# Last phase of a long-convolution gate kernel: sums of two rows in one place, row-buffer copies at the end of a step, separate buffers for x, 18 constant matmuls for 40

## The chip, the cores and the metric

The kernel runs on one core of one Trainium2 chip. The core has five engines with instruction streams of their own, which meet through semaphores: TensorE (PE, matmuls; its weight loads are shown as PEld), VectorE (DVE), ScalarE (ACT), GpSimd (POOL) and SyncE (SP, which here only issues DMAs). Sixteen DMA engines move the data of all queues. TensorE works out of SBUF, the on-chip memory, and writes to PSUM, which is read by VectorE and ScalarE. The metric is the device time of one launch, in microseconds; lower is better.

## What is computed

The reference is a long convolution (by FFT) of `x * v` with a filter that a small MLP makes from position embeddings, multiplied by `x`; then a five-tap causal convolution along the sequence, a sigmoid of it as a gate, and two 128x128 projections. Shapes: batch 4, sequence 12800, width 128.

```python
def _attn_ref(x, v, pos_emb, w1, w2):
    h_filt = (np.maximum(pos_emb @ w1, 0.0) @ w2) * np.exp(-0.01 * pos)[:, None]
    u = x * v
    L = 2 * S
    y = np.fft.irfft(np.fft.rfft(u, n=L, axis=1) * np.fft.rfft(h_filt, n=L, axis=0)[None], n=L, axis=1)[:, :S]
    return x * y
...
def _moe_ref(x, w_val, conv_w, w_out):          # x is the output of the above
    for k in range(5):
        gate_pre += conv_w[k] * xp[:, k:k + S, :]
    gate = 1.0 / (1.0 + np.exp(-gate_pre))
    return gate * (x @ w_val) @ w_out
```

## The kernel before

The FFT is cut into two halves j of 100 x 64 points (n1 x n2). The kernel has three phases, each with its own pools of SBUF and PSUM. Phase 1 makes the filter and the first transform and writes it to DRAM (`a_u`). Phase 2 goes over 50 pairs of frequencies, multiplies by the filter and transforms back along n2; it writes `c_y` to DRAM from `c_sb` (L376, L379). Phase 3, the one that changes, does the last inverse transform along n1 and everything behind it. One pool, `ld` (six buffers of 128 x 2048 words), lives through all three phases and holds what is loaded from DRAM; the pools of a phase (`p2`, `p3` and their PSUM) are given back when it ends, and the next phase's tiles take the same memory.

Phase 3 works on rows: a row is one n2 with all four batches and 100 n1, so 400 columns of 128 channels. Four rows (R = 4) make a group, 16 groups make a half, and there are 32 groups, 128 rows. The code is in `manual_schedule`: every engine runs its instructions in the order in which the Python text issues them. The loop at L591 runs over steps t, each with four rows r (L601). In step t the work is staggered over groups: group s = t + 3 goes through the inverse transform, group t through the five taps, and group t - 1 through the projections. Since the halo of the taps needs the last group of a half first, `y_order` begins each half with group 15.

In one row, these instructions are issued (names as in the profile):

- PE: four transposes `tp` (L517) of a row two rows back, the first projection `v_ps` (L554), the two inverse transforms `sd` of row (s, r) (L503, one for each half of the 128 partitions of the result), and the second projection `o_ps` (L564) of the row before. An fp32 matmul runs as two instructions in the profile, so an `sd` is shown as x4 and an `o_ps` or `v_ps` as x2.
- ACT: `dif` (L519, half of a transposed row out of PSUM), `o_sb` (L572, a result row out of PSUM), `sd_sb` (L510, the `sd` out of PSUM). In the last row of a step also the first tap of the next group (`gt`, L542) and the sigmoid (`sg`, L549).
- DVE: one of the taps 1 to 4 over the whole group (`gt`, L545), the gate times value product `gd` (L559), and the two halves `yr` of the row (L527, L528).
- POOL: `yr` times x into the row buffer `ext` or `tail` (L530).

`ext` is a buffer of 4 + 16 rows, so it holds four groups and, ahead of them, the last four rows of the four groups before. `fill_halo` (L483) copies these on ACT: L495 from the buffer before, L490 to L493 from `tail` at the start of a half, and L497 the `tail` into the end of the fourth buffer of a half. Before the change it is called in row r = 1 of a step with g % 4 == 0, eight times in all.

`load_rows` (L457) loads two tiles of `c_y` for a group, in eight DMAs on SP (96 and 4 partitions of each half tile), and the group's x with them (`load_x`, L451), one DMA. All three tiles are taken from `ld`; with six buffers that is two groups. The x of the first three groups is asked for ahead of the first `c_y` tiles (L583). While the loads run, 40 constant matmuls `w_ps` into the `o_ps` buffers (L587, called `o_ps<-dft,ident` in the profile) keep TensorE at work.

Of the kernel before, what the change touches and what calls it, by code (L numbers as in the profile page):

```python
# [9 lines left out]
F32 = mybir.dt.float32  # L10
# [13 lines left out]
B, S, D, FO, KC = 4, 12800, 128, 64, 5  # L24
J, N1, N2 = 2, 100, 64
# [1 line left out]
KG = 8  # L27
P1C = 2
R = 4
WARM = 40  # L30
NC1 = N1 // 2 + 1


# [72 lines left out]
def tile_longconv_gate(  # L106
# [56 lines left out]
    def load():  # L163
        return ld.tile([128, 2048], F32, name="ld")
# [276 lines left out]
    with tc.tile_pool(name="p3", bufs=1) as p3, tc.tile_pool(name="ps3", bufs=1, space=PSUM) as ps3:  # L441
        HALO = KC - 1
        ROW = B * N1
        NG = N2 // R
        EG = 4
# [4 lines left out]

        def load_x(s):  # L451
            j, g = y_order[s]
            xr = load()[:, 0:R * ROW]
            nc.sync.dma_start(out=xr, in_=xt[j][:, g * R:(g + 1) * R].rearrange("d n b a -> d (n b a)"))
            loads3[s] = xr

# [16 lines left out]
        def place(j, g):  # L473

            if g == NG - 1 and (j, g // EG) not in exts:
                return tails[j], 0
            return exts[j, g // EG], HALO + g % EG * R

        def new_ext(j, q):
            e = p3.tile([D, HALO + EG * R, B, N1], F32, name="ext", bufs=2)  # L480
            exts[j, q] = e
# [17 lines left out]
        def y_sum(s, r):  # L499
            ct, _ = loads3[s]  # L500
            sd = ps3.tile([128, B * D], F32, name="sd", bufs=2)
            for c in range(2):
                nc.tensor.matmul(  # L503
                    out=sd[c * N2:(c + 1) * N2], lhsT=inv[:, c], rhs=ct[c][:, r * B * D:(r + 1) * B * D],
                    start=True, stop=True)
            sds[s, r] = sd
# [15 lines left out]
        def y_join(s, r):  # L522
            tp, dif = tps.pop((s, r))
            j, g = y_order[s]
            xr = loads3[s][1].rearrange("d (n b a) -> d n b a", n=R, b=B)[:, r]
            yr = p3.tile([D, B, N1], F32, name="yr", bufs=3)
            nc.vector.tensor_tensor(yr[:, :, 0:NC1], tp[:, :, 0:NC1], dif, op=ALU.add)  # L527
            nc.vector.tensor_tensor(yr[:, :, NC1:N1], tp[:, :, 1:NC1 - 1], dif[:, :, 1:NC1 - 1], op=ALU.subtract)  # L528
            e, r0 = place(j, g)
            nc.gpsimd.tensor_tensor(e[:, r0 + r], yr, xr, op=ALU.mult)  # L530
# [24 lines left out]
            return v_ps  # L555

        def gated(t, r, v_ps):
            gd = p3.tile([D, ROW], F32, name="gd", bufs=3)
            nc.vector.tensor_tensor(gd, v_ps, gate_sg[t][:, r * ROW:(r + 1) * ROW], op=ALU.mult)  # L559
            return gd  # L560

# [18 lines left out]
        AHEAD3, NT, LAG = 3, len(groups), 2  # L580
        y_run, gd_last, o_last = [], None, None
        with tc.manual_schedule():
            for s in range(AHEAD3):  # L583
                load_x(s)
            load_rows(0)

            for _ in range(WARM):  # L587
                w_ps = ps3.tile([D, 2 * D], F32, name="o_ps", bufs=2)
                nc.tensor.matmul(  # L589
                    out=w_ps, lhsT=ident, rhs=dft.rearrange("p a k -> p (a k)"), start=True, stop=True)  # L590
            for t in range(-AHEAD3, NT + 2):  # L591
                s = t + AHEAD3
                if s + 1 < NT:
                    load_rows(s + 1)
                if 0 <= s < NT:
                    j, g = y_order[s]
                    if g == NG - 1:
                        tails[j] = p3.tile([D, R, B, N1], F32, name="tail", bufs=2)
                    elif g % EG == 0:
                        new_ext(j, g // EG)  # L600
                for r in range(R):  # L601
                    done = y_run.pop(0) if len(y_run) == LAG or s >= NT and y_run else None
                    if done:
                        y_trans(*done)
                    v_ps = value(t - 1, r) if 0 <= t - 1 < NT else None
                    if s < NT:
                        y_sum(s, r)
                    if o_last is not None:
                        finish(*o_last)
                        o_last = None  # L610
                    if gd_last is not None:
                        o_last = gd_last[0], gd_last[1], project(gd_last[2])
                        gd_last = None
                    if 0 <= t < NT:
                        tap(t, r + 1)
                    if r == R - 1 and 0 <= t + 1 < NT:
                        tap(t + 1, 0)
                    if v_ps is not None:
                        gd_last = t - 1, r, gated(t - 1, r, v_ps)
                    if done:  # L620
                        y_join(*done)
                    if s < NT:
                        y_copy(s, r)
                        y_run.append((s, r))
                    if r == R - 1 and 0 <= t < NT:
                        sigmoid(t)
                    if r == 1 and s < NT and g % EG == 0:
                        fill_halo(j, g // EG)


# [35 lines left out]
```

## Time and profile before

| | |
|---|---|
| median of 3 runs | 1285.75 us (1273.37, 1285.75, 1292.47) |
| the profiled execution | 1290.03 us; its span, first to last instruction, 1288.2 us |
| mean granted TensorE clock of it | 0.957 |
| busy in the span: PE, DVE, POOL, ACT | 91%, 79%, 67%, 49% |
| phase 3, from the first constant matmul to the end of the span | 849.5 to 1288.2 us, 438.7 us |
| busy in 850 to 1290: the taps L545, 128 instructions | 242.7 us, 1896 ns each |
| the same for L530 on POOL (into `ext`), 120 instructions | 301.6 us, 2514 ns each |

The busy share of an engine is an average over three phases with different limits, so phase 3 is read by itself, in windows and row by row. The profile gives a start and a length for each instruction. The lengths of neighbouring instructions of one engine overlap, so the pace of an engine is read from the distance of two starts, not from a length. A number in square brackets is the idle time of the engine just before the instruction, with the event that ended it.

### The profile page before, as it was taken

The page shows a single profiled execution, that of the slowest core. Times are in us where ns is not written, and L with a number is a line of the kernel's source. Part 1 is how long each engine was busy: PE and PEld are TensorE (multiplying, and loading weights), DVE is VectorE, ACT ScalarE, POOL GpSimd, SP SyncE. Part 2 cuts the span into 40 slices and gives each one's busy share as a digit, 9 for nine tenths or more (in the row PEclk, how much of TensorE's full clock was granted, in tenths as well). Part 3 has the DMA queues.
Part 4 walks back from the last instruction along what each step waited for, and adds up shares of the span by engine and source line. Part 5 has one row for each costly group of instructions (what it writes and reads, how often), then busy time and mean ns, then how long its engine had stood idle before and what let it go on. Part 6 is the DMA issues. An engine that isn't in the chain of part 4 may idle for free.

```text
span 1288.2 us, 16767 instructions
## 1 busy us (share of the span) xinstructions
PE 1174.3 (91%) x5544; PEld 572.7 (44%) x5544; DVE 1014.1 (79%) x1130; ACT 629.6 (49%) x1064; POOL 867.4 (67%) x346
## 2 busy tenths in 40 slices
PE   4869999978777899999999999989999999999996
PEld 3557776766543233333333333353344444444432
DVE  5856233797655999999999999902999899999897
ACT  3324454677533233333333333304677677667664
POOL 3324233444543689999999999913898898898790
PEclk8979999988978999999999999986999999999999
DMA  9999878889988577788777777645888988999942
GB/s 244 293 298 311 240 238 270 275 259 304 297 260 306 199 263 282 275 286 293 279 278 278 276 276 258 246 142 154 250 270 269 287 255 274 285 272 268 285 142 102
DMA packets 152254, 332.95 MB, mean 258 GB/s; under 512 B 12446, under 2 KB 64714, under 8 KB 150634
## 3 DMA queue, kind: packets, MB, share of 16 engines
q1 hardware_dynamic: 104256, 226.13, 57.8%
q10 hardware_dynamic: 47914, 105.76, 22.7%
q8 instruction: 45, 0.74, 0.2%
q14 instruction: 39, 0.32, 0.1%
HBM read 200.77 MB, written 131.07 MB: 258 GB/s over the span
## 4 chain that ended last, share of the span: by engine, by line
PE 66%; DMA 16%; DVE 8%; issue 3%; POOL 3%; ACT 3%; SPq 1%; ACTq 0%; DVEq 0%; POOLq 0%
PE c_ps L369 14%; PE z_ps L341 13%; PE sd L503 8%; DMA ld<-in_v_dram 7%; PE o_ps L564 7%; PE fp L282 7%; DMA a_u<-st 6%; PE v_ps L554 5%; PE tp L517 4%; PE z_ps L328 3%; DVE gt L545 3%; PE ap L222 2%; PE ap L221 2%; PE o_ps L589 2%; DVE vc L419 1%
## 5 line engine op out<-in xcount | busy, mean ns | idle before, releaser
L530 POOL TENSOR_TENSOR ext<-yr,ld 128x400 f32<-128x400 f32 x120 | 301.6, 2514 | 60.4 <-DVE yr L528 40.5
L259 POOL TENSOR_TENSOR u_lo<-u_t,u_hi 100x1024 fp32r<-100x1024 f32 x64 | 160.0, 2503 | 236.1 <-ACT u_hi L258 212.2
L545 DVE SCALAR_TENSOR_TENSOR gt<-ext,cw,gt 128x1600 f32<-128x1600 f32 x128 | 242.7, 1896 | 0.9 <-ACT gt L542 0.8
L376 ACT COPY c_sb<-c_ps 128x1024 f32<-128x1024 f32 x100 | 101.2, 1012 | 278.4 <-PE c_ps L369 278.4
L341 PE MATMUL z_ps<-ld 128*64 128x512 f32 x800 | 195.3, 607 | 7.7 <-DMA ld<-a_u 6.5
L428 POOL TENSOR_TENSOR va<-va,vb 128x1024 f32<-128x1024 f32 x50 | 156.9, 3138 | 37.0 <-DVE vb L346 36.9
L282 PE MATMUL fp<-u_hi,fwd_hi 100*100 100x512 f32 x256 | 116.9, 456 | 57.5 <-ACT st L285 24.7
L503 PE MATMUL sd<-ld,inv 100*64 100x512 f32 x512 | 146.1, 645 | 2.4 <-DMA ld<-c_y 2.4
L287 DVE COPY st<-fp 100x512 f32<-100x512 f32 x128 | 85.3, 685 | 65.6 <-PE fp L282 57.9
L346 DVE TENSOR_TENSOR vb<-z_ps,h_sb 128x2048 f32<-128x2048 f32 x50 | 114.5, 2291 | 24.6 <-ACT c_sb L376 24.0
L564 PE MATMUL o_ps<-gd,wout 128*128 128x400 f32 x256 | 119.5, 548 | 13.8 <-DVE gd L559 9.4
L429 POOL TENSOR_TENSOR vc<-vc,vd 128x1024 f32<-128x1024 f32 x50 | 118.2, 2365 | 18.6 <-DVE vd L346 13.7
L257 DVE TENSOR_TENSOR u_t<-ld 100x1024 f32<-100x1024 f32 x64 | 86.2, 1348 | 51.7 <-POOL u_lo L259 42.3
L346 DVE TENSOR_TENSOR va<-z_ps,h_sb 128x2048 f32<-128x2048 f32 x50 | 114.1, 2281 | 10.9 <-PE z_ps L341 10.9
L510 ACT COPY sd_sb<-sd 128x512 f32<-128x512 f32 x128 | 75.8, 592 | 88.5 <-PE sd L503 73.6
L430 POOL TENSOR_TENSOR va<-va,vb 128x1024 f32<-128x1024 f32 x50 | 118.4, 2368 | 0.0
L369 PE MATMUL c_ps<-vc,ld 64*128 64x512 f32 x400 | 102.5, 631 | 11.0 <-DVE vc L419 10.6
L282 PE MATMUL fp<-u_hi,fwd_lo 100*100 100x512 f32 x256 | 108.8, 425 | 0.0
L554 PE MATMUL v_ps<-ext,wval 128*128 128x400 f32 x256 | 107.1, 500 | 0.0
L285 ACT COPY st<-fp 100x512 f32<-100x512 f32 x128 | 70.8, 592 | 73.2 <-PE fp L282 44.2
L341 PEld LDWEIGHTS z_ps<-ld 128*64 128x64 f32 x800 | 54.6, 138 | 114.2 <-issue 85.8
L258 ACT CAST u_hi<-u_t 100x1024 fp32r<-100x1024 f32 x64 | 68.2, 1067 | 74.0 <-PE fp L282 31.8
(78 smaller groups left out, 1962.0 us busy)
## 6 DMA issues: line engine op xcount, KB each, us to landing
c_y<-c_sb ACTq DMA_DIRECT2D x100, 512.0 KB
ld<-a_u SPq DMA_DIRECT2D x49, 1024.0 KB
ld<-c_y SPq DMA_DIRECT2D x128, 384.0 KB
ld<-in_xt_dram SPq DMA_DIRECT2D x32, 800.0 KB
out_dram<-o_sb ACTq DMA_DIRECT2D x32, 800.0 KB
ld<-in_x_dram SPq DMA_DIRECT2D x64, 384.0 KB
ld<-in_v_dram SPq DMA_DIRECT2D x64, 384.0 KB
a_u<-st ACTq DMA_DIRECT2D x64, 384.0 KB
```

The source lines that it names most:

```text
L259: nc.gpsimd.tensor_tensor(lo, u_t, hi.bitcast(F32), op=ALU.subtract)
L282: nc.tensor.matmul(out=fp, lhsT=w[:, c], rhs=d[:, b:b + 2], start=(k == 0), stop=(k == 2))
L341: nc.tensor.matmul(out=z[half[h]], lhsT=wk[:, h, half[c]], rhs=a2[:, h, j], start=True, stop=True)
L346: nc.vector.tensor_tensor(out, z.rearrange("p (b d) -> p b d", d=D).unsqueeze(1).to_broadcast([128, n, B, D]), h_sb.unsqueeze(2).to_broadc ...
L369: nc.tensor.matmul(out=c_ps[:, h], lhsT=wk[half[h], 2 + c], rhs=vt[half[h], c].rearrange("p b d -> p (b d)"), start=(c == 0), stop=(c == 1))
L428: nc.gpsimd.tensor_tensor(va[:, 0:2], va[:, 0:2], vb[:, 0:2], op=ALU.add)
L430: nc.gpsimd.tensor_tensor(va[:, 2:4], va[:, 2:4], vb[:, 2:4], op=ALU.add)
L503: nc.tensor.matmul(out=sd[c * N2:(c + 1) * N2], lhsT=inv[:, c], rhs=ct[c][:, r * B * D:(r + 1) * B * D], start=True, stop=True)
L530: nc.gpsimd.tensor_tensor(e[:, r0 + r], yr, xr, op=ALU.mult)
L545: nc.vector.scalar_tensor_tensor(gt, rows(t, k), cw[:, k:k + 1], gt, op0=ALU.mult, op1=ALU.add)
L554: nc.tensor.matmul(out=v_ps, lhsT=wval, rhs=rows(t)[:, r * ROW:(r + 1) * ROW], start=True, stop=True)
L564: nc.tensor.matmul(out=o_ps, lhsT=wout, rhs=gd, start=True, stop=True)
```

## The change

Five things change in phase 3.

1. `sd` of rows r and r + 1 are issued together in the even rows, behind `o_ps` in place of ahead of it; the odd rows have none.
2. `fill_halo` is called in row 3 of the step in place of row 1.
3. x gets two buffers `xr` in the pool of phase 3; `ld` then holds `c_y` tiles alone, of three groups. Only two x are asked for ahead of the first rows.
4. `yr` and `gd` have two buffers in place of three.
5. 18 constant matmuls in place of 40.

```diff
-WARM = 40
+WARM = 18
...
-            xr = load()[:, 0:R * ROW]
+            xr = p3.tile([D, R * ROW], F32, name="xr", bufs=2)
...
-            yr = p3.tile([D, B, N1], F32, name="yr", bufs=3)
+            yr = p3.tile([D, B, N1], F32, name="yr", bufs=2)
...
-            gd = p3.tile([D, ROW], F32, name="gd", bufs=3)
+            gd = p3.tile([D, ROW], F32, name="gd", bufs=2)
...
-            for s in range(AHEAD3):
+            for s in range(2):
                 load_x(s)
...
                     v_ps = value(t - 1, r) if 0 <= t - 1 < NT else None
-                    if s < NT:
-                        y_sum(s, r)
                     if o_last is not None:
                         finish(*o_last)
                         o_last = None
                     if gd_last is not None:
                         o_last = gd_last[0], gd_last[1], project(gd_last[2])
                         gd_last = None
+                    if s < NT and r % 2 == 0:
+                        y_sum(s, r)
+                        y_sum(s, r + 1)
...
-                    if r == 1 and s < NT and g % EG == 0:
+                    if r == R - 1 and s < NT and g % EG == 0:
                         fill_halo(j, g // EG)
```

On PE, two rows in the middle of the phase read so before (`tp_` with a number is the transposed row, x4 its four batches):

```order
L517 MATMUL tp_6879<-ident,sd_sb 128x128 x4
L554 MATMUL v_ps<-ext,wval 128x400
L503 MATMUL sd<-ld,inv 64x512 x2
L564 MATMUL o_ps<-gd,wout 128x400
L517 MATMUL tp_6919<-ident,sd_sb 128x128 x4
L554 MATMUL v_ps<-ext,wval 128x400
L503 MATMUL sd<-ld,inv 64x512 x2
L564 MATMUL o_ps<-gd,wout 128x400
```

and so now:

```order
L517 MATMUL tp_6924<-ident,sd_sb 128x128 x4
L554 MATMUL v_ps<-ext,wval 128x400
L564 MATMUL o_ps<-gd,wout 128x400
L503 MATMUL sd<-ld,inv 64x512 x4
L517 MATMUL tp_6952<-ident,sd_sb 128x128 x4
L554 MATMUL v_ps<-ext,wval 128x400
L564 MATMUL o_ps<-gd,wout 128x400
```

Both projections now follow each other in every row, and four `sd` stand in one run in every second row.

On SP, at the start of the phase, before (what a row waits for stands in brackets: DMAHW is an earlier DMA of a queue, PE and Pool are engines that still use the buffer):

```order
L454 DMA ld<-in_xt_dram 128x1600 [waits DMAHW7_49,DMAHW2_49,PE_49]
L454 DMA ld<-in_xt_dram 128x1600 [waits DMAHW5_49,DMAHW2_49,PE_49]
L454 DMA ld<-in_xt_dram 128x1600 [waits DMAHW5_49,DMAHW1_49,PE_49]
L102 DMA ld<-c_y 96x1024 [waits DMAHW4_49,DMAHW3_49,DMAHW6_49,DMAHW1_49,DMAHW7_49,DMAHW0_49,PE_49]
L102 DMA ld<-c_y 4x1024 [waits DMAHW4_49,DMAHW3_49,DMAHW5_49,DMAHW2_49,DMAHW1_49]
```

and now:

```order
L454 DMA xr<-in_xt_dram 128x1600 [waits DMAHW3_49,DMAHW4_49,DMAHW2_49,DMAHW5_49,DMAHW1_49,DMAHW6_49,DMAHW0_49,DMAHW7_49,DVE_49,Activation_49]
L454 DMA xr<-in_xt_dram 128x1600
L102 DMA ld<-c_y 96x1024
L102 DMA ld<-c_y 4x1024
L102 DMA ld<-c_y 96x1024
```

The first x now lies in memory of phase 2, so its load waits for all of phase 2's DMAs and for DVE and ACT, and the `c_y` loads stand behind it in the queue. Further on, the `c_y` tiles of groups 1 and 2 wait for no engine any more; before, the second tile of group 1 waits for PE (it takes a buffer of group 0) and the second of group 2 for POOL (it takes that of the first x).

On ACT, around a copy between row buffers, before:

```order
L519 COPY dif<-tp_7058 128x204
L572 COPY o_sb<-o_ps 128x400
L575 DMA out_dram<-o_sb 128x1600
L510 COPY sd_sb<-sd 128x512
L495 COPY ext<-ext 128x1600
L519 COPY dif<-tp_7084 128x204
```

and now:

```order
L519 COPY dif<-tp_7067 128x204
L572 COPY o_sb<-o_ps 128x400
L542 ACTIVATE gt<-ext,cw 128x1600
L510 COPY sd_sb<-sd 128x512
L549 ACTIVATE sg<-gt 128x1600
L495 COPY ext<-ext 128x1600
L519 COPY dif<-tp_7105 128x204
```

The copy has moved behind the sigmoid of the step, two rows later, and now stands ahead of the `dif` of the next step's first row.

## The prediction

> **What bounds it now.** I read the windows of the last phase first, then the chain of waits in order of time, then the timeline of one row. Columns of a window: stretch, length, busy time of PE, PEld, DVE, ACT, POOL, granted clock, DMA share, GB/s.
>
> ```profile
> 900.00:935.00 35.00, 32.24 (x136) 13.22 (x134) 31.89 (x43) 22.79 (x38) 28.70 (x12) 0.98 0.83 239
> 935.00:1012.00 77.00, 77.00 (x312) 32.76 (x312) 74.71 (x109) 53.67 (x94) 68.80 (x28) 1.00 0.90 271
> ```
>
> PE never stops and DVE nearly so. Two rows of the chain give the pace of PE, three its end:
>
> ```profile
> 1031.65 1.01 PE sd L503 x4
> ...
> 1205.02 1.01 PE sd L503 x4
> ...
> 1261.02 1.87 DVE gt L545
> 1263.29 1.87 DVE gt L545
> ...
> 1274.76 1.79 DVE gt L545
> ```
>
> From 1031.65 to 1205.02 there are 58 rows, so 2.99 us a row, and the chain runs over PE. Where `sd` and `yr` have ended, DVE carries it, at 2.27 us a row. One row in the middle:
>
> ```profile
> 952.91 0.20 PEld L503 LDWEIGHTS sd<-ld,inv 100*64 100x64 f32 x4 [0.57 <-PE tp L517]
> 952.91 1.08 PE L503 MATMUL sd<-ld,inv 100*64 100x512 f32 x4
> 952.96 1.88 DVE L545 SCALAR_TENSOR_TENSOR gt<-ext,cw,gt 128x1600 f32<-128x1600 f32 x1
> 953.13 2.61 POOL L530 TENSOR_TENSOR ext<-yr,ld 128x400 f32<-128x400 f32 x1 [0.21 <-DVE yr L528]
> 953.92 0.30 PEld L564 LDWEIGHTS o_ps<-gd,wout 128*128 128x128 f32 x2 [0.81 <-ACT o_sb L572]
> 953.92 0.94 PE L564 MATMUL o_ps<-gd,wout 128*128 128x400 f32 x2
> 954.36 0.14 PEld L517 LDWEIGHTS tp<-ident,sd_sb 128*128 128x128 f32 x1
> 954.70 0.60 PE L517 MATMUL tp<-ident,sd_sb 128*128 128x128 f32 x4
> 954.75 0.57 DVE L559 TENSOR_TENSOR gd<-v_ps,sg 128x400 f32<-128x400 f32 x1
> 955.02 0.30 PEld L554 LDWEIGHTS v_ps<-ext,wval 128*128 128x128 f32 x2
> 955.13 0.84 PE L554 MATMUL v_ps<-ext,wval 128*128 128x400 f32 x2
> 955.24 0.37 DVE L527 TENSOR_TENSOR yr<-tp,dif 128x204 f32<-128x204 f32 x1
> 955.78 1.88 DVE L545 SCALAR_TENSOR_TENSOR gt<-ext,cw,gt 128x1600 f32<-128x1600 f32 x1
> 955.90 1.08 PE L503 MATMUL sd<-ld,inv 100*64 100x512 f32 x4
> ```
>
> By starts, PE spends 1.01 on `sd`, 0.78 on `o_ps`, 0.43 on `tp`, 0.77 on `v_ps`: 2.99. DVE goes from tap to tap in 2.82, POOL moves with it. So PE is 0.17 us a row slower than DVE. The reader is to see the weight loads too: those of `tp` and `v_ps` begin ahead of their matmuls, while the preceding ones run; those of `sd` and `o_ps` begin together with theirs, after 0.57 and 0.81 of idle time. The releaser named for `o_ps` had long been done; the load stands behind the `sd` matmuls.
>
> **The pair of sums.** Per two rows PE now has tp, v, o, sd, sd, tp, v, o. A run of two `sd` is seen at the start of the phase:
>
> ```profile
> 869.10 1.94 PE L503 MATMUL sd<-ld,inv 100*64 100x512 f32 x8
> ...
> 870.97 0.66 PE L517 MATMUL tp<-ident,sd_sb 128*128 128x128 f32 x4
> ...
> 871.55 1.08 PE L503 MATMUL sd<-ld,inv 100*64 100x512 f32 x4
> ```
>
> The run takes 1.87, for 2.02 in two pieces. `v_ps` followed by `o_ps` on a busy PE the trace doesn't show. Upper bound: every step costs what it costs now, 0.43 + 0.77 + 0.77 + 1.87 + 0.58 (a `tp` between sums, 870.97 to 871.55) + 0.77 + 0.78 = 5.97, no gain. Lower bound: no load shows. `tp` streams 512 columns in 0.43, so the 2 x 400 of a projection take 0.67: 2 x 0.43 + 4 x 0.67 + 1.87 = 5.41. I take the lower one plus 0.10 for the load of `sd` (0.77 - 0.67, as behind `v_ps` now) and half of the 0.15 that a `tp` beside sums costs: 5.59, or 2.80 a row, since a 128-column load ahead of `tp` and `v_ps` is hidden today. That is just under DVE's 2.82, so DVE sets the pace. DMA bears it: a step moves two `c_y` tiles of 100 x 2048, x and the output of 128 x 1600 words, 3.28 MB; 271 GB/s at a share of 0.90 makes 301 at most, 10.9 us, against 4 x 2.82 = 11.28. `o_ps` now waits for `gd` ahead of the sums, which costs nothing as long as DVE is the bound; what is queued behind it are the sums, whose PSUM buffers ACT has emptied a row earlier.
>
> What it gives: the first tap starts at 900.86 (row below), the last at 1274.76, so with one more pitch 376.2 us. DVE alone needs 116 rows x 2.82 + 12 x 2.27 = 354.4. Of the 21.8 between them I leave 3.1, the idle time of DVE in 900 to 935, when the groups start.
>
> **The copies.** Before, a copy on ACT waits for POOL, and with it all that stands behind it on ACT:
>
> ```profile
> 1025.97 1.53 ACT L495 COPY ext<-ext 128x1600 f32<-128x1600 f32 x1 [1.95 <-POOL ext L530]
> ...
> 1027.41 1.52 ACT L497 COPY ext<-tail 128x1600 f32<-128x1600 f32 x1
> ```
>
> In row 3 the wait for POOL is gone, but the copy stands behind ACT's longest row:
>
> ```profile
> 955.33 0.33 ACT L519 COPY dif<-tp 128x204 f32<-128x204 f32 x1 [0.69 <-DVE gd L559]
> ...
> 955.94 1.64 ACT L542 ACTIVATE gt<-ext,cw 128x1600 f32<-128x1600 f32 x1
> ...
> 959.38 0.34 ACT L519 COPY dif<-tp 128x204 f32<-128x204 f32 x1
> ```
>
> From `dif` to the next `dif` are 4.05. With DVE as the bound, row 3's `dif` comes at best at 0.57 + 0.77 + 1.87 + 0.63 = 3.84 after row 1's `gd` starts (`gd`, `o_ps`, the pair, and `tp` 954.70 to `dif` 955.33). The next is done at 3.84 + 4.05 + 0.33 = 8.22; DVE wants it at 3 x 2.82 + 0.49 = 8.95. One copy of 1.53 makes it 0.8 late, two make it 2.3. After the start there are five steps with one copy (or small ones of that sum) and two with two: 8.6 us. Both ends: 0, if DVE has time left there, to 7 x 1.53 + 2 x 1.52 = 13.8. So the steady part gives 21.8 - 3.1 - 8.6 = 10.1, with ends 0 and 21.8.
>
> **Fewer buffers.** POOL reads `yr` until 955.74 (953.13 + 2.61) and the buffer is wanted again at the second `yr` behind it, over 2 us later; `gd` is read within the next row. Nothing.
>
> **The start.** x and 40 matmuls:
>
> ```profile
> 849.47 19.70 PE L589 MATMUL o_ps<-dft,ident 128*128 128x256 f32 x80 [1.10 <-ACT c_sb L376]
> 853.62 38.27 SPq L102 DMA_DIRECT2D ld<-c_y  x31
> ...
> 878.18 1.94 PE L503 MATMUL sd<-ld,inv 100*64 100x512 f32 x2 [2.37 <-DMA ld<-c_y]
> ...
> 884.05 1.98 PE L503 MATMUL sd<-ld,inv 100*64 100x512 f32 x4
> ...
> 885.96 1.12 PE L517 MATMUL tp<-ident,sd_sb 128*128 128x128 f32 x4
> ...
> 887.00 1.98 PE L503 MATMUL sd<-ld,inv 100*64 100x512 f32 x4
> ...
> 900.86 1.97 DVE L545 SCALAR_TENSOR_TENSOR gt<-ext,cw,gt 128x1600 f32<-128x1600 f32 x1 [0.82 <-ACT gt L542]
> ```
>
> ```profile
> 852.00:854.00 2.00, 2.00 (x6) 1.55 (x6) 0.00 (x0) 0.00 (x0) 0.00 (x0) 0.53 0.50 192
> ...
> 876.00:878.00 2.00, 0.00 (x0) 0.00 (x0) 0.00 (x0) 0.00 (x0) 0.95 (x1) 0.94 1.03 299
> 878.00:880.00 2.00, 1.82 (x2) 0.29 (x2) 0.00 (x0) 0.00 (x0) 0.00 (x0) 0.50 1.04 264
> ...
> 900.00:902.00 2.00, 2.00 (x8) 0.91 (x8) 1.18 (x2) 1.51 (x3) 1.03 (x1) 0.58 0.17 29
> ```
>
> Now the constant matmuls hold back the first sum until 869.10, and group 1 waits at 878.18 for a tile that had no buffer. In that wait the clock falls to 0.50, and stays there until about 901.7, 23.5 us, though PE works all the time; a row then costs 1.91 + 1.04.
>
> After: 36 instructions, about ten of them up to 854 at the low clock and the rest at 15.1 / 70 = 0.22 us, end at 859.6. But both x now wait until 853.62 and go first: 1.64 MB, then 1.23 MB of `c_y` for the first row, at 264 GB/s, 10.9 us, so the first `sd` is at about 866 with the landing. PE has idled 6 us, and the clock is low. The first tap comes after 12 `sd`, 10 `tp`, `dif` and the first tap on ACT: 12 x 1.91 + 10 x 1.04 + 0.33 + 1.64 = 35.3, at 901.3, if the clock stays low. If it is low for 23.5 us again, until 889.5, the last 9.8 of PE's 33.3 us halve: 896.4, 4.5 us earlier than now. I take this, from the one low stretch under this pattern. The ends: 0.4 later, and the DMA limit: both x and three groups are 6.55 MB, landed at 878.4, and about 8 us of fast sums and taps behind them, 887, so 14 earlier.
>
> The Trainium skill ("TensorE: Matmul & The Clock Gate", Part 1) says that the clock halves after an idle window of about 3.4 us and comes back after about 3.4 us of sustained matmuls; its section "Why this matters for your kernels" advises against gaps over about 3 us, so it speaks against the shorter run of constant matmuls. The fall agrees with the 0.94 and 0.50 above; the return does not, 23.5 us here. By the page the start would end near 887, the second rival's figure.
>
> **The sum.** 1290.0 - 10.1 - 4.5 = 1275.4 against the profiled execution, which lies 4.3 above the median of the three runs (1285.75): 1271.
>
> **Rivals.** (a) The clock comes back soon, since two sums in one run keep PE denser: the start gives 14, 1290.0 - 10.1 - 14 - 4.3 = 1262. For it: 854, when it rose under dense matmuls; against: the 23.5 us. (b) PE's upper bound holds (loads show behind `v_ps` too), or DMA can't exceed 271 GB/s (3.28 MB then take 12.1 us a step): the steady part gives nothing, 1290.0 - 4.5 - 4.3 = 1281. Against: the hidden loads of `v_ps`, and 299 GB/s in one window. (c) Slower: the gap at 859.6 leaves the clock low far into the taps. There two rows cost 2 x 5.59 in place of 5.64, half a microsecond for each one, so beyond about 921 it eats the 9.7 that the steady part and a start 0.4 later leave. Two stretches of 23.5 from 866 end at 913 and don't; a third, until 936.5, costs 17.6: 1290.0 - 10.1 + 0.4 + 17.6 - 4.3 = 1294. For it: the clock did not come back by itself under sums and transposes for one stretch; against: it did after one.
>
> **Chances.** Forecast 0.50 (1262 to 1281), (a) 0.18, (b) 0.26, (c) 0.06. The range 1255 to 1288 takes in the forecast, (a) and (b) with some 7 us about them, and leaves out (c) and the case in which all bounds are at their best together (1290.0 - 21.8 - 14 - 4.3 = 1250). 2% (25.7 us) is about what a measurement tells from no change here: under 1260 lie half of (a) and a tenth of the forecast, 0.15; over 1311.5 lies (c) with more than four stretches, 0.02.
>
> **What would show it.** Right: `sd` pairs 5.64 apart, `gt` starts 2.82 apart nearly without idle time on DVE, `o_ps` waiting for `gd`, and DVE waiting for `dif` only in the steps with copies. Wrong: pairs 5.97 apart, a wait for `c_y` or x in the middle, or a clock of 0.5 behind the first tap.

## The result, and the profile after

| | before | after |
|---|---|---|
| median of 20 runs each | 1288.74 us (1273.37 to 1300.30) | 1270.68 us (1256.93 to 1281.72) |
| ratio, after to before | | 0.986, 95% interval 0.9823 to 0.9897 |
| the profiled execution, its span | 1290.03, 1288.2 us | 1275.39, 1273.6 us |
| first constant matmul (end of phase 2) | 849.5 | 855.1 |
| from there to the first tap L545 on DVE | 51.4 | 37.9 |
| first tap to last tap | 373.8 | 367.0 |
| behind the last tap's start | 13.6 | 13.6 |
| phase 3 | 438.8 | 418.5 |

The kernel is 1.4% faster, 18.1 us by the medians. The ratios here and below leave out, of both kernels, the executions more than 1.5% above the fastest of the same kernel, so they need not be the ratios of the medians. The lower part of the table is read from the starts in the two traces, and it is cleaner than the totals: phases 1 and 2 are the same instructions in all kernels here (but for the load of the first x in e5 and e9), yet the traces of this study end them anywhere between 845.5 and 861.5 us. Between the two profiled executions that is 5.6 us against the change; the start of phase 3 gives 13.5, the part between the taps 6.8: 14.7 in all, the spans' 1288.2 - 1273.6 but for rounding.

The windows of the last phase after the change, columns as before (length, busy PE, PEld, DVE, ACT, POOL, granted clock, DMA share, GB/s):

```profile
893.00:935.00 42.00, 36.41 (x152) 16.52 (x152) 40.25 (x53) 27.18 (x47) 31.21 (x15) 1.00 0.99 267
935.00:1012.00 77.00, 76.33 (x326) 35.04 (x326) 76.01 (x109) 54.22 (x94) 70.17 (x27) 1.00 0.93 282
```

In 935 to 1012 PE issues 326 matmuls where it had 312, and DVE is busy for 76.01 in place of 74.71. One pair of rows in the timeline of the changed kernel:

```profile
957.17 1.87 DVE L545 SCALAR_TENSOR_TENSOR gt<-ext,cw,gt 128x1600 f32<-128x1600 f32 x1
...
957.69 1.94 PE L503 MATMUL sd<-ld,inv 100*64 100x512 f32 x8
...
959.56 0.66 PE L517 MATMUL tp<-ident,sd_sb 128*128 128x128 f32 x4
...
959.99 1.88 DVE L545 SCALAR_TENSOR_TENSOR gt<-ext,cw,gt 128x1600 f32<-128x1600 f32 x1
960.05 0.84 PE L554 MATMUL v_ps<-ext,wval 128*128 128x400 f32 x2
...
960.73 0.83 PE L564 MATMUL o_ps<-gd,wout 128*128 128x400 f32 x2
...
961.40 0.60 PE L517 MATMUL tp<-ident,sd_sb 128*128 128x128 f32 x4
...
961.78 0.56 DVE L559 TENSOR_TENSOR gd<-v_ps,sg 128x400 f32<-128x400 f32 x1
961.83 0.84 PE L554 MATMUL v_ps<-ext,wval 128*128 128x400 f32 x2
...
962.46 0.30 PEld L564 LDWEIGHTS o_ps<-gd,wout 128*128 128x128 f32 x2 [0.44 <-issue]
962.51 0.90 PE L564 MATMUL o_ps<-gd,wout 128*128 128x400 f32 x2
...
962.81 1.87 DVE L545 SCALAR_TENSOR_TENSOR gt<-ext,cw,gt 128x1600 f32<-128x1600 f32 x1
...
963.33 0.20 PEld L503 LDWEIGHTS sd<-ld,inv 100*64 100x64 f32 x4 [0.57 <-issue]
963.34 1.94 PE L503 MATMUL sd<-ld,inv 100*64 100x512 f32 x8
```

By starts, the run of `sd` takes 1.87, the first `o_ps` behind `v_ps` 0.67, and from one run of `sd` to the next it is 5.65. The taps stand 2.82 apart. `o_ps` begins 0.17 behind the end of `gd` (961.78 + 0.56): PE follows DVE. In the chain of waits the runs of `sd` stand that far apart too:

```profile
1197.79 1.87 PE sd L503 x8
1203.43 1.87 PE sd L503 x8
```

Where a copy stands, DVE waits. Two copies in one step, in the timeline of DVE before the change:

```profile
1024.96 0.57 DVE L559 TENSOR_TENSOR gd<-v_ps,sg 128x400 f32<-128x400 f32 x1
1029.25 0.37 DVE L527 TENSOR_TENSOR yr<-tp,dif 128x204 f32<-128x204 f32 x1 [3.73 <-ACT dif L519]
```

and after it, a single copy on ACT and the wait on DVE, then the same for two copies:

```profile
971.54 0.33 ACT L519 COPY dif<-tp 128x204 f32<-128x204 f32 x1 [0.82 <-PE tp L517]
...
975.59 1.53 ACT L495 COPY ext<-ext 128x1600 f32<-128x1600 f32 x1
977.00 0.35 ACT L519 COPY dif<-tp 128x204 f32<-128x204 f32 x1
...
977.45 0.37 DVE L527 TENSOR_TENSOR yr<-tp,dif 128x204 f32<-128x204 f32 x1 [0.99 <-ACT dif L519]
...
1020.40 1.55 ACT L549 ACTIVATE sg<-gt 128x1600 f32<-128x1600 f32 x1
1021.84 1.53 ACT L495 COPY ext<-ext 128x1600 f32<-128x1600 f32 x1
1023.25 1.54 ACT L497 COPY ext<-tail 128x1600 f32<-128x1600 f32 x1
1024.68 0.34 ACT L519 COPY dif<-tp 128x204 f32<-128x204 f32 x1
...
1025.12 0.37 DVE L527 TENSOR_TENSOR yr<-tp,dif 128x204 f32<-128x204 f32 x1 [2.41 <-ACT dif L519]
```

The wait for `dif` falls from 3.73 to 2.41 in a step with two copies, and a single copy costs 0.99 (2.29 before, at 980.21). The starts of the taps show something that the prediction did not use. A step of four taps took 11.29 before the change too, except at the copies:

| tap steps (us) | no copy | one copy | start of a half | two copies |
|---|---|---|---|---|
| before | 11.29 (11.44 once) | 13.68 to 13.81 | 13.89 | 15.18, 15.99 |
| after | 11.29 (four steps of 12.0 to 12.4, see e12) | 12.37 (12.65 once) | 12.68 | 13.79, 13.80 |

PE meanwhile kept its 11.96 from the `sd` of one group to that of the next, except at two copies (12.91 and 13.66). So before the change DVE lost 2.4 to 4.7 at a copy, and in the three steps between it ran at its own pace, faster than PE's. Four steps with one copy take DVE 4 x 11.29 + 2.4 = 47.6 and PE 4 x 11.96 = 47.8: two bounds of nearly the same size lay over each other, and that is what most of the experiments are about.

The start of the phase after the change, on PE and on SP:

```profile
855.05 9.95 PE L589 MATMUL o_ps<-dft,ident 128*128 128x256 f32 x36 [1.10 <-ACT c_sb L376]
867.57 1.04 PE L503 MATMUL sd<-ld,inv 100*64 100x512 f32 x2 [2.57 <-DMA ld<-c_y]
871.33 3.68 PE L503 MATMUL sd<-ld,inv 100*64 100x512 f32 x6 [2.72 <-DMA ld<-c_y]
874.94 1.12 PE L517 MATMUL tp<-ident,sd_sb 128*128 128x128 f32 x4
875.98 1.94 PE L503 MATMUL sd<-ld,inv 100*64 100x512 f32 x8
...
859.12 0.82 SPq L454 DMA_DIRECT2D xr<-in_xt_dram  x2
859.99 20.92 SPq L102 DMA_DIRECT2D ld<-c_y  x24
```

```profile
869.00:871.00 2.00, 0.00 (x0) 0.00 (x0) 0.00 (x0) 0.00 (x0) 0.00 (x0) 0.55 1.04 234
...
873.00:876.00 3.00, 3.00 (x10) 0.96 (x7) 0.00 (x0) 1.17 (x2) 0.00 (x0) 0.50 1.05 265
876.00:878.00 2.00, 2.00 (x10) 0.62 (x10) 0.64 (x2) 0.92 (x2) 0.69 (x1) 1.00 1.02 240
```

PE waits for `c_y` twice, the clock is low from 869.2 to 876.0 (6.8 us, where it was 23.9 before), and all three groups are asked for in one go of 21 us while the DMA share stays between 0.94 and 1.06. (The share counts a transfer whole where it starts, so a short stretch can show more than 1.)

### The profile page after: what moved, and what is told of

Its sections match the earlier page's. It is cut to its first block, busy times and chain, and to the rows that moved or that the text cites. A ratio compares the mean times of both kernels' runs of the same rounds, so it can differ in the third digit from the quotient of the medians.

```text
span 1273.6 us, 16726 instructions
## 1 busy us (share of the span) xinstructions
PE 1144.7 (90%) x5500; PEld 570.2 (45%) x5500; DVE 1018.0 (80%) x1130; ACT 628.3 (49%) x1064; POOL 862.4 (68%) x346
## 5 line engine op out<-in xcount | busy, mean ns | idle before, releaser
L530 POOL TENSOR_TENSOR ext<-yr,xr 128x400 f32<-128x400 f32 x120 | 298.1, 2486 | 48.9 <-DVE yr L528 46.5
L545 DVE SCALAR_TENSOR_TENSOR gt<-ext,cw,gt 128x1600 f32<-128x1600 f32 x128 | 242.6, 1895 | 1.8 <-ACT gt L542 1.8
L503 PE MATMUL sd<-ld,inv 100*64 100x512 f32 x512 | 129.8, 611 | 10.6 <-DMA ld<-c_y 9.1
L564 PE MATMUL o_ps<-gd,wout 128*128 128x400 f32 x256 | 112.0, 519 | 18.3 <-DVE gd L559 10.7
L369 PE MATMUL c_ps<-vc,ld 64*128 64x512 f32 x400 | 100.7, 622 | 14.6 <-DVE vc L419 14.5
```

Source lines behind the costliest of these rows:

```text
L503: nc.tensor.matmul(out=sd[c * N2:(c + 1) * N2], lhsT=inv[:, c], rhs=ct[c][:, r * B * D:(r + 1) * B * D], start=True, stop=True)
L545: nc.vector.scalar_tensor_tensor(gt, rows(t, k), cw[:, k:k + 1], gt, op0=ALU.mult, op1=ALU.add)
L564: nc.tensor.matmul(out=o_ps, lhsT=wout, rhs=gd, start=True, stop=True)
```

## The experiments

All times in us, read as in the table above; the ratio is to the kernel before on the same chip. The first three columns are of the one profiled execution of each.

| run | to first tap | first to last tap | phase 3 | median (runs) | ratio to before, 95% |
|---|---|---|---|---|---|
| before, after | 51.4, 37.9 | 373.8, 367.0 | 438.8, 418.5 | above | above |
| e1_single_sums | 44.7 | 370.1 | 428.3 | 1281.76 (12) | 0.9933, 0.988 to 0.9987 |
| e2_copy_row1 | 43.9 | 373.6 | 431.1 | 1275.66 (6) | 0.9899, 0.9832 to 0.9965 |
| e3_warm40 | 37.1 | 365.8 | 416.5 | 1266.86 (6) | 0.9833, 0.9769 to 0.9897 |
| e4_copy_spread | 38.8 | 357.3 | 409.7 | 1270.48 (6) | 0.9861, 0.9791 to 0.9931 |
| e5_x0_early | 37.3 | 363.5 | 414.4 | 1270.94 (4) | 0.9899, 0.9811 to 0.9987 |
| e6_pair_only | 47.7 | 372.6 | 433.9 | 1282.17 (10) | 0.9985, 0.9941 to 1.003 |
| e7_warm18_only | 36.3 | 373.8 | 423.7 | 1273.25 (10) | 0.9953, 0.9897 to 1.0009 |
| e8_buffers_only | 37.4 | 377.3 | 428.2 | 1279.38 (10) | 0.9938, 0.9887 to 0.9989 |
| e9_spread_x0 | 36.2 | 353.8 | 403.5 | 1264.74 (6) | 0.9858, 0.98 to 0.9915 |
| e10_before_spread | 46.4 | 369.4 | 429.3 | one run | |
| e11_no_first_x | 31.5 | 363.1 | 408.2 | one run | |
| e12_after_again | 37.5 | 363.5 | 414.5 | 1269.94 (6) | 0.9897, 0.9835 to 0.996 |

### The steady part: sums and copies

**e1_single_sums**, the changed kernel with the sums one by one at their old place:

```diff
+                    if s < NT:
+                        y_sum(s, r)
...
-                    if s < NT and r % 2 == 0:
-                        y_sum(s, r)
-                        y_sum(s, r + 1)
```

> The changed kernel with the sums of a row back in their old place, one row at a time ahead of o_ps; everything else as changed. Theory (the pair is what makes PE fast enough): PE's row is 2.99 us again, a step 11.96, and from the first tap to the last 375 us in place of the 367.0 of the changed kernel's profile (373.8 before the change); DVE idles 0.17 us a row; total 7 to 9 us above the changed kernel's 1270.7, about 1279. The start too may lose, if the clock comes back later without the pairs: up to 8 us more. Rival (the pace came with the own buffers of x and the deeper loads of c_y): the step stays 11.29 and the time within 2 us of 1270.7.

The taps take 370.1 from first to last, where 375 was expected, 3.7 less than before the change, and `sd` goes at 11.96 a step: the change without the pairs gives 3.7 here, and then PE's single sums are the bound. The start does lose, 6.8 (44.7 for 37.9): the clock was low for 23.9 behind the constants.

**e2_copy_row1**, the changed kernel with the copies back in row 1:

```diff
-                    if r == R - 1 and s < NT and g % EG == 0:
+                    if r == 1 and s < NT and g % EG == 0:
```

> The changed kernel with the copies between row buffers back in row 1. Theory: DVE is the bound now, so what DVE waits for dif at a copy is lost. In the profile before, DVE's step was 2.4 us too long at a step with one copy and 3.9 at one with two (13.69 and 15.18 for 11.29); in the changed kernel 1.09 and 2.5. So this one is slower by 5 x 1.3 + 2 x 1.4 = 9 us, about 1279.5, with steps of some 13.7 and 15.2 us at the copies. Rival (the place of the copies does nothing, as the old 11.96 us step hid them): within 2 us of 1270.7.

373.6: 6.5 of the 6.8 is lost again, though the sums are in pairs. Some 1.0 of it stands in two late steps (11.77 and 11.82): PE waited 2.70 at a step with two copies (`o_ps` at 1209.97), and the clock fell for 3.4 at 1211.0. The steps with copies take 13.67 to 13.89 and 15.10, as expected.

**e6_pair_only**, the kernel before with the sums in pairs behind `o_ps` and nothing else (the edit of e1 the other way round):

> The kernel before with the sums in pairs behind o_ps, nothing else changed. Theory: PE's pairs of rows are 5.64 apart as DVE allows, and DVE then loses 2.4 and 3.9 us at the copies in row 1, so from the first tap to the last about 373 us, as before (373.8); in the start the low clock lasts 2 to 4 windows of 3.4 us in place of 7, so the first tap comes 45 to 48 us after the first constant matmul in place of 51.4. Total 4 to 7 us below the kernel before. Rival (the pair brings the steady part 17 us, 104 rows of 0.17): from tap to tap 357.

372.6 against 373.8. Sums in pairs, alone, give 1.2 in the steady part, and the total is not shown to move (0.9985, 0.9941 to 1.003). The timeline of DVE in this run shows why; it is that of before, to 0.01:

```profile
1024.97 0.56 DVE L559 TENSOR_TENSOR gd<-v_ps,sg 128x400 f32<-128x400 f32 x1
1029.26 0.37 DVE L527 TENSOR_TENSOR yr<-tp,dif 128x204 f32<-128x204 f32 x1 [3.72 <-ACT dif L519]
```

**e4_copy_spread**, the changed kernel with the copies cut into single rows (at the start of a half: into its three stripes), one piece behind `sd_sb` in each of the rows 0 to 2 that follow:

```diff
-                nc.scalar.copy(out=e[:, 0:HALO], in_=exts[j, q - 1][:, EG * R:])
+                p = exts[j, q - 1]
+                pieces = [[(e[:, k:k + 1], p[:, EG * R + k:EG * R + k + 1])] for k in range(HALO)]
...
-                    if r == R - 1 and s < NT and g % EG == 0:
+                    if r == 2 and s < NT and g % EG == 0:
                         fill_halo(j, g // EG)
+                    if todo and r < R - 1:
+                        copy_piece()
```

> The changed kernel with each copy cut into four rows of 400 columns (at the start of a half into its column pieces), one in each of rows 2, 0, 1, 2 behind sd_sb, none in row 3. Theory: ACT has the time in these rows, so DVE waits for dif no more and the long steps of 12.37 and 13.80 us fall to 11.29: 1.1 x 4 + 1.4 + 2 x 2.5 = 10.8 us, from the first tap to the last 356 to 359 us, total 1260. Rival (something else holds DVE at these steps, POOL or the loads): the long steps stay, and the time within 3 us of 1270.7.

357.3, 9.7 less than the changed kernel in its profile and 6.2 less than in its second (e12). The tap steps with copies now take 11.29 as well, but for 0.2 and 0.8 at the start of the second half. DVE has no idle time left:

```profile
935.00:1012.00 77.00, 77.00 (x329) 35.76 (x329) 77.00 (x109) 55.91 (x101) 71.22 (x28) 1.00 0.95 292
```

The total does not show it: the median, 1270.48, was expected at 1260 and is that of the changed kernel, 1270.68, which ran on another chip.

**e10_before_spread**, the same pieces in the kernel before, with the sums one by one:

> The kernel before with one edit: the copies cut into single rows, one piece in each of rows 0 to 2, sums one by one as before. Theory of two bounds of nearly equal size (PE 2.99 a row, DVE 2.82 a row plus the copies): PE's single sums now bind alone, sd steps of 11.96, first to last tap 369 to 371, no better than with whole copies in row 3 (370.1). Rival (the copies cost what they cost, 16.3 us as between copies in row 1 and spread copies with sums in pairs, whatever the sums do): 373.8 - 16.3 = 357 to 358.

369.4, and 11.96 a step for `sd` throughout, so the theory of two bounds holds. Its windows and a piece of its timeline (its lines lie eight further down than those of the profile before):

```profile
929.00:1006.00 77.00, 77.00 (x311) 32.75 (x310) 76.19 (x106) 51.97 (x95) 63.62 (x27) 1.00 0.93 281
```

```profile
960.47 2.41 DVE L553 SCALAR_TENSOR_TENSOR gt<-ext,cw,gt 128x1600 f32<-128x1600 f32 x1 [0.38 <-ACT gt L550]
```

PE is full, and DVE now waits for the chain behind PE (here for the first tap on ACT) where it used to wait for a copy. Copies spread are worth 4.4 with single sums (373.8 to 369.4) and 16.3 with sums in pairs (e2 to e4, 373.6 to 357.3, of which 1.0 is the low clock in e2); pairs are worth 1.2 with the copies in row 1 (e6) and 12.1 with spread ones (e10 to e4, which differ in the buffers and the constants too). Neither part has a price of its own.

### The start: loads and clock

**e7_warm18_only**, the kernel before with WARM = 18:

> The kernel before with 18 constant matmuls, nothing else changed. Theory: the first group of c_y lands about 10 us after the first constant matmul, so the first sum starts there in place of 19.6, and the wait of group 1 for a buffer comes as much earlier; with the same low stretch of 24 us the first tap comes at 42 in place of 51.4, and the total falls by 9. Rival (the tile of group 1, not the constants, sets the first tap): 49 to 51, total unchanged.

36.3: earlier than the theory's 42, since the clock was low for 6.8 and not for 24. The total is not shown to be lower (0.9953, 0.9897 to 1.0009).

**e8_buffers_only**, the kernel before with the separate buffers for x and two of `yr` and `gd`:

```diff
-            xr = load()[:, 0:R * ROW]
+            xr = p3.tile([D, R * ROW], F32, name="xr", bufs=2)
...
-            for s in range(AHEAD3):
+            for s in range(2):
```

> The kernel before with the own buffers of x (two for yr and gd), nothing else changed: 40 constants, single sums, copies in row 1. Theory: at the end of the constants the first group is there and the next ones follow without a wait for a buffer, so PE does not idle for a window and the clock stays up: first tap 38 to 42 us after the first constant matmul in place of 51.4; from tap to tap 373 to 375. Total 9 to 12 us below the kernel before. Rival (the gain of the start came with the fewer constants): first tap at 48 to 51.

The first tap comes at 37.4, but the taps take 377.3, where 373 to 375 was expected: PE now waits for `c_y` around the first taps.

```profile
891.50 1.04 PE L503 MATMUL sd<-ld,inv 100*64 100x512 f32 x2 [2.23 <-DMA ld<-c_y]
...
902.01 1.04 PE L503 MATMUL sd<-ld,inv 100*64 100x512 f32 x2 [2.41 <-DMA ld<-c_y]
```

So of the 14.0 that the first tap comes earlier, phase 3 keeps 10.5.

**e3_warm40**, the changed kernel with WARM = 40:

> The changed kernel with 40 constant matmuls. Theory: they end some 19.3 us after their start, at about which time all of the first group has landed, and the clock stays up, so that the first tap comes 38 to 40 us after their start, against 37.9 in the changed kernel's profile: total 0 to 3 us above 1270.7, perhaps below it where the clock had stayed low. Rival (the 22 matmuls less are worth their own time, 44 x 0.216 us): 9.5 us above, 1280.

The first tap comes 36.3 us behind the first constant matmul with the fewer constants alone, 37.4 with the buffers alone, 37.9 with both, and 37.1 with all of the change but the fewer constants. Against the 51.4 of before each is worth 14 or 15 by itself, and together they are worth no more. That 51.4 is one execution: e10 and e6, which start with the constants and buffers of before, had 46.4 and 47.7, and against these each is worth 9 to 11. With the buffers, 18 constants for 40 gain nothing: in e3 the first `sd` comes 4.9 later than in the changed kernel (17.5 against 12.5 behind the first constant matmul), PE then waits for no load before the first tap, the clock stays up until then, and the first tap comes 0.8 earlier.

**e5_x0_early**, the changed kernel with the first x in a buffer of its own that no earlier phase has used, and the second x behind the `c_y` of group 1:

```diff
+    xrp = ctx.enter_context(tc.tile_pool(name="xrp", bufs=1))
...
-            xr = p3.tile([D, R * ROW], F32, name="xr", bufs=2)
+            xr = xrp.tile([D, R * ROW], F32, name="x0") if s == 0 else p3.tile([D, R * ROW], F32, name="xr", bufs=2)
...
-            for s in range(2):
-                load_x(s)
+            load_x(0)
```

> The changed kernel with the first x in a buffer that is free in phase 2, so that its load runs before the phase, and the second x asked for behind the loads of c_y of group 1. Theory (the two x ahead of c_y delay the first sums by their transfer time, 1.64 MB or 6.2 us, and the first tap by what is still ahead of the third group, 0.82 MB or 3.1 us less): from the first constant matmul to the first sum 6 to 9 us in place of 12.2 to 12.6, to the first tap 3 us less than with the changed order at the same stretch of low clock (37.9 and 38.8 in two profiles). Rival (DMA is not what holds the start): first tap as before, 38 to 39.

The first `sd` does come 4.5 earlier (8.0 behind the first constant matmul), the first tap only 0.6, for the 3 expected. The time saved ahead is waited for later: `sd` at 876.86 waits 2.59 for `c_y`.

**e11_no_first_x**, the changed kernel without x in the first three groups; POOL multiplies `yr` by itself in those 12 rows, so it still works as long:

```diff
-            for s in range(2):
-                load_x(s)
...
-            if s not in loads3:
+            if s >= AHEAD3:
                 load_x(s)
-            loads3[s] = ct, loads3[s]
+            loads3[s] = ct, loads3.get(s)
...
+            xr = yr if s < AHEAD3 else loads3[s][1].rearrange("d (n b a) -> d n b a", n=R, b=B)[:, r]
```

> The changed kernel without x in the first three groups (POOL multiplies yr by itself there, so those 12 rows are not the reference's); 2.46 MB less are loaded at the start. Theory (the loads hold the first tap at 36 to 38 us after the first constant matmul, at some 280 GB/s): 2.46 MB less are 8.8 us, first tap at 28 to 31, where PE's 12 sums and 10 transposes behind the first tile become the bound. Rival (the low clock or PE's own work behind the first sum holds it): 35 to 38 as in the changed kernel. The steady part is unchanged, 365 to 368.

31.5, 6.0 to 6.4 less than the changed kernel and 0.5 above what was expected. With 2.46 MB less the first group is there sooner, the waits for `c_y` are of one microsecond or less, and the clock never falls:

```profile
855.64 1.07 PE L503 MATMUL sd<-ld,inv 100*64 100x512 f32 x2
857.25 1.90 PE L503 MATMUL sd<-ld,inv 100*64 100x512 f32 x6 [0.54 <-DMA ld<-c_y]
...
864.64 1.90 PE L503 MATMUL sd<-ld,inv 100*64 100x512 f32 x6 [1.00 <-DMA ld<-c_y]
...
871.79 1.90 PE L503 MATMUL sd<-ld,inv 100*64 100x512 f32 x6 [0.33 <-DMA ld<-c_y]
```

```profile
856.00:879.00 23.00, 21.04 (x95) 8.60 (x94) 6.43 (x21) 12.00 (x25) 8.16 (x10) 1.00 1.01 251
```

So the loads have a part in the start, and the rival, that the clock or PE's own work alone holds it, falls. But the loads alone do not hold it either, as the theory had it. The following table takes the start apart at the `sd` of the second row (behind the first constant matmul), by which PE has what it first needs of group 0:

| run | second row | from there to the first tap | PE busy in it | granted clock in it | busy x clock |
|---|---|---|---|---|---|
| before | 20.5 | 30.85 | 28.48 | 0.63 | 17.9 |
| e10_before_spread | 20.4 | 25.95 | 23.37 | 0.80 | 18.7 |
| e7_warm18_only | 11.2 | 25.12 | 22.52 | 0.86 | 19.4 |
| e8_buffers_only | 18.4 | 19.02 | 17.80 | 1.00 | 17.8 |
| after | 17.2 | 20.73 | 19.96 | 0.91 | 18.2 |
| e1_single_sums | 16.5 | 28.19 | 28.19 | 0.62 | 17.5 |
| e2_copy_row1 | 16.6 | 27.33 | 24.55 | 0.74 | 18.2 |
| e3_warm40 | 18.4 | 18.71 | 18.19 | 1.00 | 18.2 |
| e5_x0_early | 10.9 | 26.40 | 22.55 | 0.87 | 19.6 |
| e11_no_first_x | 10.0 | 21.43 | 20.01 | 1.00 | 20.0 |

The last column, PE's work as it would be at the full clock, is 17.4 to 20.0 in all traces. What differs is when it begins, how long PE waits within it, and the clock. The loads set when it begins: at 17.2 with both x ahead of `c_y`, at 10.0 without them (and the constants do, at 18.4, where 40 of them stand ahead). The clock decides as much: e1 and e2 have the buffers, the constants and the loads of the changed kernel and begin at 16.5 and 16.6, yet their first taps come at 44.7 and 43.9, at a clock of 0.62 and 0.74. e3 and e8 lose nothing to the clock, and there PE is busy nearly all the time. That so many starts end at 36 to 38 is no common limit.

### The two together, and the changed kernel again

**e9_spread_x0**, the edits of e4 and e5 together:

> The changed kernel with two more edits put together: the copies between row buffers cut into single rows, one piece in each of rows 0 to 2 of the steps, and the second x loaded behind the c_y tiles of group 1. Theory (DVE sets the pace and the copies were what was left; the start is held by DMA from the first loads on): first constant matmul to first tap 36 to 38, first to last tap 354 to 358, phase 3 403 to 410 us against 418.5 of the changed kernel, median 1258 to 1264. Rival (the row pieces and the earlier load take DMA or ACT time from each other): first to last tap 362 or more, phase 3 above 412, median 1267 or more.

Phase 3 takes 403.5 us, 15.0 less than the changed kernel in its first profile and 11.0 less than in its second (e12), the shortest of all. The tap steps are 11.29 from the third on, except around the start of the second half (11.52 and 12.09). The median, 1264.74, is 0.7 above the expected stretch and 5.2 below that of the changed kernel on the same chip; with six runs each, the two intervals overlap, so by the totals it is not shown to be the faster one; by phase 3 it is, in one trace of each.

**e12_after_again**, the changed kernel unaltered:

> The changed kernel unaltered, on the same chip as the three others, for the comparison of totals. Theory (only phase 3 differs, 418.5 against 438.8 us; the two phases ahead of it differ from run to run): phase 3 416 to 421 again, whatever the time of the phases ahead; median 1267 to 1274. Rival (part of the 20 us lies in how the phases fell in the one profiled execution): phase 3 outside of 413 to 424.

Phase 3 took 414.5, 1.5 below the theory's stretch, but not outside of 413 to 424, as the rival had it. Of the difference of 4.0 from the first profile 3.5 lies between the taps, 363.5 against 367.0: five steps that took 0.3 to 1.1 more in the first profile, three at the start of the phase and two near 1147. At the start the waits for `c_y` were longer (PE 2.00 and 1.83 at 894.44 and 904.71, ACT 3.77 at 922.95; in e12 1.55, 0.83 and 2.48). One of the two near 1147 reads so on the first profile's timeline:

```profile
1141.61 0.50 ACT L572 COPY o_sb<-o_ps 128x400 f32<-128x400 f32 x1
1145.26 0.34 ACTq L575 DMA_DIRECT2D out_dram<-o_sb  x1
1145.64 0.59 ACT L510 COPY sd_sb<-sd 128x512 f32<-128x512 f32 x1 [3.53 <-DMA ld<-c_y]
...
1146.28 1.08 PE L503 MATMUL sd<-ld,inv 100*64 100x512 f32 x4 [0.79 <-ACT sd_sb L510]
...
1146.56 0.37 DVE L527 TENSOR_TENSOR yr<-tp,dif 128x204 f32<-128x204 f32 x1 [0.31 <-ACT dif L519]
```

and on ACT in e12, at the same place of the program:

```profile
1146.04 0.34 ACTq L575 DMA_DIRECT2D out_dram<-o_sb  x1
1146.42 0.59 ACT L510 COPY sd_sb<-sd 128x512 f32<-128x512 f32 x1 [0.41 <-ACT o_sb L572]
```

ACT issues the output's DMA, and by the releaser of the row behind it that issue waits until an earlier load of `c_y` has landed; behind it stands `sd_sb`, for which the second `sd` waits, and in the end DVE. In e12 the loads were done in time. e4 shows such delays at two steps, one step earlier in the program (0.6 and 0.7, behind an ACT wait of 3.45 at 1131.66); e9 and e11 don't.

## Why the prediction came out as it did

The time, 1271, was right, in part by luck. The forecast gain was 14.6, from a median before of 1285.75 in three runs; the measured one is 18.1, from 1288.74 in twenty. The sum for the profiled execution (1275.4, measured 1275.39) was right by more than its terms deserve. Against them, the start gave 9.0 more, the steady part 3.3 less, and the phases ahead, which the sum took as equal, ended 5.6 later.

- **The pair, 5.59 by a value between two bounds.** Right: the run of `sd` is the 1.87 that was taken from the start of the phase, `o_ps` behind `v_ps` the 0.67 without a load, and PE's pair is 5.65 when it has to follow DVE's 5.64. That is at most 0.06 above the estimate; PE and DVE are so close that e4's windows show both full (77.00 of 77.00), and the traces don't tell how much room PE has left. DVE sets the pace at 2.82, as forecast. Rival (b), that PE stays at 5.97 or DMA can't exceed 271 GB/s, fell on both counts: 5.65, and 282 GB/s.
- **The steady part, 10.1.** Right in size for the kernel, 3.3 too much for its first profile: 6.8 there, 10.3 in e12 (373.8 - 363.5), 10.7 in e11. The 3.5 between the profiles is, by the waits in the two traces, the loads' lateness, which the prediction named only as a sign that it would be wrong ("a wait for `c_y` or x in the middle") and had given no price.
- **The copies, 8.6.** The mechanism was right, `dif` behind a copy in ACT's longest row, and two copies cost 2.5 for the forecast 2.3. The single one was mis-sized, 1.08 for 0.8, and the start of the second half cost 1.39. In all 4 x 1.08 + 1.39 + 2 x 2.5 = 10.7. The step that was off is "3.84 after row 1's `gd` starts": it is 4.11 (`gd` at 967.43, `dif` at 971.54), since `o_ps` starts 0.72 behind the start of `gd` and not 0.57, and then keeps `sd` back for 0.83. DVE's idle time beside the copies was put too high in turn: 363.5 - 352.1 - 10.7 = 0.7 in e12 for 3.1 (352.1 is the prediction's 354.4 less the last tap's 2.27).
- **What the steady part's reasoning lacked.** It credited the whole gain to the pair and entered the copies as a loss within it. Before the change the copies already held DVE up for 21 us (the seven steps of the table, less 11.29 each), which with its 352.1 makes 373: DVE's own bound was 373 and PE's, by e1 and e10, 369 to 370. e6 and e1 show that neither edit gives the 10 (pairs alone 1.2, the change without them 3.7); together they give more than the two apart, because each leaves only the other's bound.
- **The start, 4.5.** Wrong in size: 13.5. The first `sd` was forecast 16.5 behind the first constant matmul and came at 12.5. The step that failed is "if it is low for 23.5 us again ... I take this, from the one low stretch under this pattern". In the changed kernel the clock was low for 6.8, and with 6.8 in place of 23.5 the prediction's own sum gives 866 + 6.8 + (33.3 - 6.8) / 2 + 2.0 = 888.0, 12.8 earlier. Against the profile before, the second row begins 3.3 earlier and what follows it takes 10.1 less: some 8.7 by the clock (28.48 x 0.37 less 19.96 x 0.09) and 1.6 by shorter waits. The stretch does not belong to the pattern. The kernel of e10 starts with the same sums, constants and loads as the one before. Its PE meets the same wait,

```profile
875.77 1.94 PE L511 MATMUL sd<-ld,inv 100*64 100x512 f32 x2 [2.58 <-DMA ld<-c_y]
```

but there the clock was low for 10.2 in place of 23.9, and the first tap came at 46.4 in place of 51.4. The other end of the range, the DMA limit at 887, which is 37.5 behind the first constant matmul, agrees with what was measured (37.9, and 37.5 in e12) by luck: it has three groups land first and 8 us of work behind them, while PE waits for the first group alone (2.57 and 2.72) and then, from 871.33 to 892.4, for no load. Rival (a), a clock that comes back soon, is what happened, and its 14 was near. Its reason, that pairs keep PE denser, is not shown: with single sums the clock was low for 23.9 in e1 and not at all in e8, with pairs for 13.7 in e2.
- **Fewer constants.** The prediction gave them no term apart from the rest of the start, and by e3 there is none beside the buffers. Alone (e7) they bring the first tap as far forward as the buffers alone (e8), 36.3, by another way: the second row begins at 11.2, DMA is not full (0.73 from 866 to 892), and PE waits 2.60 for a `c_y` tile and works at a low clock for 6.8.
- **Rival (c)**, a clock that stays low far into the taps, did not occur as such. At the start the latest low window ended at 912.5, in e6, a single one; but in e2 the clock fell once in the middle of the taps, for one window at 1211.0, and two steps lost 1.0 by it.
- **Fewer `yr` and `gd` buffers, nothing.** No row of the changed kernel's timeline above waits for one. They were not undone by themselves.

The Trainium skill's rule ("TensorE: Matmul & The Clock Gate", Part 1), a fall after an idle window of about 3.4 us and a return after about as much work, gives the start nearly as measured, but the traces bear out only part of its cause. Some low stretches end after one window of 3.4 (e3, e6, e9), as the rule says. Those of 23.9 in the kernel before and in e1 don't, under sums and transposes without a gap. And the falls came behind waits of PE of 1.8 to 2.8 us by the profile's rows (2.37 in the kernel before), shorter than that window, so the prediction's "the fall agrees" is too strong. (The 887 that it calls the second rival's figure is that of rival (a).)

What stays open: why the low clock lasts for three windows in one execution and for seven in another of the same start, whether the pairs shorten it, and how much of the median's 18.1 is the start, since the start of before itself was seen at 46.4 and at 51.4.

## What to carry to other kernels

Where two engines are within some per cent of each other, read the starts of the second one step by step: if it runs at its own pace between hiccups, the hiccups are its bound, and removing them alone or speeding up the first engine alone gives little (3.7 or 4.4, and 1.2, where the two together gave 10 to 16). Price such edits in both orders, or as a pair. At the start of a phase, take the time apart: when the first loads are there, the engine's own work behind them, its waits, and the clock in it. Several starts that end at the same time need not have the same limit. And look for DMA issues that may wait for a load on an engine that others wait for; moving the one found here was not tried.

## What the runs showed of the hardware

- The low clock comes in whole windows of 3.413 us. The stretches behind the constant matmuls lasted 3.4, 6.8, 10.2, 13.7 or 23.9 us, that is 1, 2, 3, 4 or 7 windows. With the sums one by one seven windows were seen twice (before, e1), three once (e10), two once (e7) and none once (e8); with sums in pairs never more than four. What such a stretch costs is seen in the table of the start: between the second row and the first tap PE was busy for 28.19 us at a clock of 0.62 in e1, and for 18.19 at full clock in e3.
- The clock fell behind waits of PE of 1.8 to 2.8 us, but not behind each of them: in e2 one of 2.70 (`o_ps` at 1209.97) was followed by a fall and one of 2.71 (`o_ps` at 1018.11) was not, and in e8 neither 2.23 nor 2.41 was.
- DMA moved 282 GB/s over 77 us at a share of 0.93 and 292 at 0.95, beside full PE and DVE, where the kernel before had moved 271 at 0.90.
- An instruction that only issues a DMA held ACT for 3.5 us, while it waited, by the profile, for a load that another engine had issued.
